# Closing the last attention run in two halves and feeding the residual into PSUM: two token-mixing layers on one Trainium2 core

## The chip, the cores and the metric

The kernel runs on one core of one Trainium2 chip. The core has five engines that work side by side and are held together by semaphores: PE (TensorE, the matrix unit, with its weight loads shown apart as PEld), DVE (VectorE), ACT (ScalarE), POOL (GpSimd) and SP (SyncE, which here only issues DMAs). The metric is the device time of one launch in microseconds, the median of several runs.

## The reference, cut to what matters

```python
S, D, H, F = 2048, 640, 32, 1536          # one sequence, heads of 20 columns

def A(x):                                  # attention on a layer-normed input
    q, k, v = heads(x @ wqkv)
    p = softmax(q @ k.T / sqrt(20))
    return heads_back(p @ v) @ wo

def B(x):                                  # a token-mixing MLP, along the sequence
    h = layernorm(x)
    u = gelu(einsum("sd,sf->df", h, w1) + b1)
    return (einsum("df,fs->ds", u, w2) + b2).T

x = A_x
x = x + A(layernorm(x));  x = x + B(layernorm(x))
x = x + A(layernorm(x));  x = x + B(layernorm(x))      # the same weights again
```

B mixes along the sequence: no row of its output is known before the last row of its input is. So each attention stage must be finished to the last token before the mixer's nonlinearity can start, and this happens twice, once per layer. The two layernorms in front of B are folded into one normalization with a slightly different epsilon (`twice=True`).

## The kernel before

**Attention.** The function `attention` runs once per layer. The 2048 queries are cut into blocks of 512, the 32 heads into 8 groups of 4 heads (one per 32 rows of PE). A *run* is one query block with one group; it consists of 16 *units*, each a stretch of 128 keys. For every unit PE makes the scores (tile `S`, line 643), ACT takes the exponential (tile `P`, line 705), and PE multiplies by V into the PSUM tile `acc` (line 1177), whose extra column holds the denominator. A part of the exponentials is computed on DVE instead of ACT, by integer tricks, in pairs of 512-column chunks (`ve_admit`, lines 542 to 602). Whether a pair is given to DVE is decided while the program is written out, by a planner that keeps estimated clocks of the engines and a DVE backlog; the result is a fixed order of instructions.

**The last query block** is worked in two halves of 256 queries. In its runs the 16 units are two times 8: units 0 to 7 belong to group 2g and write columns 0 to 255 of `acc`, units 8 to 15 belong to group 2g+1 and write columns 256 to 511 (function `spans`).

**Closing a run** (`finish_run`): DVE transposes `acc` (line 733), takes the reciprocal of the denominators (746), scales (749) and transposes back into `attnT` (755). There is a single `acc` bank, so the next run's products wait for the first of these four steps. After the last closing, `enqueue_outproj_last` multiplies `attnT` by `wo` (line 1006) and adds the residual on DVE into the SBUF tile `x1last` (line 1014). For the last half block the first three of its four pairs of groups are projected while attention still runs; only the last pair is left for after the end.

**Between attention and mixer.** `emit_ln2_staged` then normalizes the last two tiles of 128 tokens on DVE: two `bn_stats` each (lines 195, 196), `bn_aggr` (198), the variance plus epsilon (201), the power on POOL (206), and the application (882) into `h2_view`. Before that it makes ACT load the table for GELU (879). Meanwhile PE multiplies zeros (`zero_wave`, line 695), 18 waves of four matmuls, to stay busy.

**The mixer.** All but the last two token tiles have been multiplied by `w1` during attention, in groups of matmuls (line 921) whose results DVE copies out (930) and POOL adds up in DRAM by DMA (`uacc`, 938). `mixer_head` adds the rest: for each of 12 row tiles, PE multiplies the last two token tiles (line 1602, tile `um`), DVE adds the partial sum that SP loaded back from `uacc` (load 1587, addition 1605), ACT applies GELU (1608), and PE starts on the products with `w2` (1624, later 1615). In the first layer the loaded sums lie in `KT`, in the second in `ua`. SP's queue is served in order; in the second layer it holds, in this order, `w2s` for tiles 0 and 1, the loads of `ua` 0 to 7, `w2s` for tiles 2 and 3, the loads of `ua` 8 to 11, and then the residual `x1in`.

Of the kernel before, what the change touches and what calls it, by code (L numbers as in the profile page):

```python
# [12 lines left out]
BF16 = mybir.dt.bfloat16  # L13
F32 = mybir.dt.float32
# [9 lines left out]
D = 640  # L24
H = 32
DH = 20
# [39 lines left out]
HOLD = 3  # L66
WARM_WAVES = 18
LOG2E = 1.4426950408889634
# [9 lines left out]
def kernel(  # L78
# [108 lines left out]
    def setup_wo():  # L187
        for h in range(H):
            g, j = divmod(h, 4)
            nc.sync.dma_start(out=wo_pad[32 * j:32 * j + DH, g, :], in_=A_wo[h * DH:(h + 1) * DH, :])  # L190

    def ln_stats(src, twice=False):
        st = stat.tile([128, 2, nc.vector.BN_STATS_DIM], F32, name="bnst")
        half = D // 2
        nc.vector.bn_stats(out=st[:, 0, :], in_=src[:, 0:half])
        nc.vector.bn_stats(out=st[:, 1, :], in_=src[:, half:D])
        mv = stat.tile([128, nc.vector.BN_AGGR_DIM], F32, name="mv")
        nc.vector.bn_aggr(out=mv[:], in_=st[:])
        veps = stat.tile([128, 1], F32, name="veps")
        if twice:  # L200
            nc.vector.tensor_scalar(out=veps[:], in0=mv[:, 1:2], scalar1=1.0 + LN_EPS, scalar2=LN_EPS * LN_EPS,
                                    op0=ALU.mult, op1=ALU.add)
        else:
            nc.vector.tensor_scalar_add(out=veps[:], in0=mv[:, 1:2], scalar1=LN_EPS)
        rstd = stat.tile([128, 1], F32, name="rstd")
        nc.gpsimd.tensor_tensor(out=rstd[:], in0=veps[:], in1=mhalf[:], op=ALU.pow)
        return mv[:, 0:1], rstd[:, 0:1]

# [22 lines left out]
    def attention(st, x_in_ap, x_mid, uacc_l, feed, feed_stack):  # L231
# [165 lines left out]
        def new_run(qb, g, final, closed):  # L397
            run = dict(qb=qb, g=g, pending=[], done=0, closed=closed, final=final, acc=None)
            runs.append(run)
            return run  # L400
# [29 lines left out]
        def extend(now):  # L430
# [3 lines left out]
            if all(reach(qg, now) == NKT - ptr[qg] for qg in early_runs):  # L434
                early[0] = False
                for qg in sorted(early_runs, key=lambda qg: (cur is None or qg != (cur["qb"], cur["g"]), qg)):
# [11 lines left out]
                    run["final"] = run["closed"] = True  # L448
                for qg in order_left:
                    run = new_run(*qg, True, True)  # L450
                    for kt in range(NKT):
                        add_unit(run, kt)
                return True
            if cur is not None and reach((cur["qb"], cur["g"]), now) == 0:
# [262 lines left out]
        def finish_run(run):  # L717
# [3 lines left out]
            acc_free[0] = 1e9  # L721
            box = {}
            nth = part_no.get((qb, g), 0)
            whole = run["final"]
# [3 lines left out]
            def turn(end):  # L728
                if not whole and nth == 0:
                    box["T1"] = part_view((qb, g))  # L730
                else:
                    box["T1"] = ntmp.tile([128, 512], F32, name="T1")[:]
                nc.vector.transpose(out=box["T1"], in_=acc[:])  # L733
                acc_free[0] = end + DVE_TO_PE
# [8 lines left out]
            def recip(end):  # L743
                box["v"] = box["T1"].rearrange("p (c i) -> p c i", i=32)
                box["r"] = ntmp.tile([128, 16], F32, name="rden")
                nc.vector.reciprocal(out=box["r"][:], in_=box["v"][:, :, DH])

            def scaled(end):
                nc.vector.tensor_tensor(out=T2[:, :, 0:DH], in0=box["v"][:, :, 0:DH],
                                        in1=box["r"][:].unsqueeze(2).to_broadcast([128, 16, DH]), op=ALU.mult)  # L750

            def back(end):
                to = late["atp"].tile([128, 512], BF16, name="attnT")
                at_live[0] += 1
                nc.vector.transpose(out=to[:], in_=T2[:].rearrange("p c i -> p (c i)"))
                attnT_tiles.setdefault(qb, {})[g] = to

            def after(end):
                early_left.discard((qb, g))
                if qb >= LASTQB:  # L760
                    last = NG // 2 - 1
                    if qb == LASTQB and g == last:
                        enqueue_outproj_last(0, list(range(NG // 2)), end + DVE_TO_PE)
                    elif qb > LASTQB and g == last - 1:
                        enqueue_outproj_last(1, list(range(last)), end + DVE_TO_PE)
                    elif qb > LASTQB and g == last:
                        enqueue_outproj_last(1, [last], end + DVE_TO_PE)
                elif len(attnT_tiles[qb]) == NG:
                    enqueue_outproj(qb, end + DVE_TO_PE)
            rest = [(0.5, added, 0.0, True)] if nth else []  # L770
            if whole:
                rest += [(0.244, recip, 0.0), (0.49, scaled, 0.0, True), (0.71, back, 0.0)]
            ahead = [p for p in dvm["procs"] if p.rank in (0, 3) and getattr(p, "norm", False)]
            first = Proc(0, [(0.71, turn, 0.0)], at + PE_TO_DVE)

# [17 lines left out]
        hT_dead = [False]  # L793
        ln2_deferred = []
        N_KEYS = 2 * NQB * NG
# [60 lines left out]
        def do_ln2(tt, x1s, end):  # L856
            if tt >= NT - TAIL:
                ln2_deferred.append((tt, x1s))
                return

            def dst():
# [14 lines left out]

        def emit_ln2_staged(items):
            assert check_hT_dead()
            nc.scalar.activation(out=warm_act[:, 0:1], in_=mhalf[:, 0:1], func=ACT.Gelu_apprx_tanh, scale=1.0)
            stats = [ln_stats(x1s[:], twice=True) for (tt, x1s) in items]  # L880
            for (tt, x1s), (mean, rstd) in zip(items, stats):
                nc.vector.tensor_scalar(out=h2_view[:, tt, :], in0=x1s[:], scalar1=mean, scalar2=rstd,
                                        op0=ALU.subtract, op1=ALU.mult)

# [103 lines left out]
        def enqueue_outproj_last(half, pairs, ready):  # L988
            attnT = attnT_tiles[LASTQB + half]
            first, final = pairs[0] == 0, pairs[-1] == NG // 2 - 1  # L990
            tt0 = 4 * LASTQB + 2 * half
            if first:
                load_xin(tt0)
            if half == 0:
                mm1_prefetch(NQB - 2, 0)
            for ttl in range(2):
                tt = tt0 + ttl
                for ci, (c0, c1) in enumerate(((0, D // 2), (D // 2, D))):
# [3 lines left out]
                    for gi, (gp, odd) in enumerate(gs):  # L1002
                        def mm(t, gp=gp, odd=odd, gi=gi, ttl=ttl, c0=c0, c1=c1, w=w, ci=ci, tt=tt):
                            if first and gi == 0 and ci == 0 and ttl < 1:
                                load_xin(tt + 1)
# [6 lines left out]
                    def evac(t, end, eng, tt=tt, c0=c0, c1=c1, w=w, ci=ci):  # L1012
                        x1s = x1last[:, tt - 4 * LASTQB, :]
                        nc.vector.tensor_tensor(out=x1s[:, c0:c1], in0=t[:, 0:w],
                                                in1=tt_state[tt]["xin"][:, c0:c1] if first else x1s[:, c0:c1], op=ALU.add)
                        if first and ci == 1:
                            del tt_state[tt]
                        if final and ci == 1:
                            do_ln2(tt, x1s, end)
                    add_fill("O", 500.0, mms, evac, w, ready=ready)  # L1020
# [292 lines left out]
        assert not dvm["procs"] and not acm["procs"]  # L1313
        emit_ln2_staged(ln2_deferred)
        idle = pp["acc"].tile([128, 512], F32, name="acc")
# [422 lines left out]
```

## Time and profile before

| | |
|---|---|
| median of 3 runs | 1787.47 us (1786.66 to 1788.98) |
| the profiled execution | 1791.82 us, of which the span from first to last instruction is 1789.6 us |
| mean granted TensorE clock | 0.993 |
| PE busy | 1702.3 us, 95% of the span |
| ACT busy | 1680.8 us, 94%; of it 1640.2 us are exponentials (line 705) |
| DVE busy | 1542.4 us, 86% |
| POOL busy | 360.1 us, 20% |
| last exponential ends, first layer and second | 830.2 and 1716.8 us |
| first addition in the mixer's head (line 1605), first layer and second | 840.64 and 1727.37 us |

Times in the profile are counted from the first instruction of the profiled execution. A line of a timeline gives the start in us, the duration in us, the engine, the source line, the operation, what it writes and reads, and how often; in brackets stands the idle time of the engine before it and what ended that. A line of the windows view gives, for each stretch, its length, the busy time and the number of instructions of each engine, and then the granted clock of PE, the mean busy share of the 16 DMA engines, and GB/s. The DMA share counts packets in flight, so it can stand a little over 1.

### The profile page before, as it was taken

What the parts mean: (1) busy time and instruction counts of PE and PEld (TensorE: products, weight loads), DVE (VectorE), ACT (ScalarE), POOL (GpSimd) and SP (SyncE); (2) the same over time, 40 slices, a digit from 0 to 9 for tenths busy, and PEclk for the clock granted to TensorE, in tenths of its full rate; (3) what the DMA queues carried; (4) which work ended last, traced back from release to release, by engine and by line L of the source; (5) the groups of instructions that cost most, each with busy time, mean ns of one, the idle gap of its engine ahead of it and who ended that gap; (6) DMA issues with size and microseconds to landing.
All of it is one profiled execution on the core that took longest, in us unless ns stands there. A gap on an engine that the chain in (4) does not pass through costs nothing.

```text
span 1789.6 us, 42888 instructions
## 1 busy us (share of the span) xinstructions
PE 1702.3 (95%) x17880; PEld 669.4 (37%) x17880; DVE 1542.4 (86%) x2433; ACT 1680.8 (94%) x1508; POOL 360.1 (20%) x539
## 2 busy tenths in 40 slices
PE   8999999999999999999999998999999999999999
PEld 3333333333333344444533432333333333444445
DVE  7479999999999999998543478999999999899972
ACT  8999999999999999997789998999999999899960
POOL 3011111122233121231000011112223331212310
PEclk9999999999999999999999998999999999899999
DMA  4200000011225110057412100001212440101665
GB/s 121 27 1 1 1 2 2 23 51 55 70 53 93 21 46 2 10 88 202 140 50 73 61 1 1 1 2 38 65 49 82 85 73 2 61 2 36 100 212 180
DMA packets 110306, 97.56 MB, mean 55 GB/s; under 512 B 52128, under 2 KB 88608, under 8 KB 110112
## 3 DMA queue, kind: packets, MB, share of 16 engines
q1 hardware_dynamic: 97664, 71.22, 13.2%
q0 software_dynamic: 12448, 23.61, 7.9%
q8 instruction: 139, 2.28, 0.5%
q14 instruction: 55, 0.45, 0.1%
HBM read 55.48 MB, written 39.32 MB: 53 GB/s over the span
## 4 chain that ended last, share of the span: by engine, by line
ACT 48%; PE 24%; issue 21%; DVE 6%; DMA 1%; SPq 0%; POOL 0%; DVEq 0%; ACTq 0%; POOLq 0%
ACT P L705 48%; PE S L643 7%; PE acc L1177 3%; PE misc L921 2%; PE acc L695 2%; PE ya L1615 2%; PE misc L1028 1%; DVE ew L542 1%; DVE et L576 1%; DVE Pd L585 1%; PE um L1602 1%; PE ya L1624 1%; PE yb L1615 1%; DVE ey L572 1%; PE misc L968 0%
## 5 line engine op out<-in xcount | busy, mean ns | idle before, releaser
L705 ACT ACTIVATE P<-S 128x1024 bf16<-128x1024 f32 (+1 forms) x1450 | 1640.2, 1371 | 22.8 <-PE S L643 17.2
L643 PE MATMUL S<-QTq,KT 32*128 32x512 bf16 (+1 forms) x4528 | 589.0, 338 | 67.8 <-ACT P L705 51.2
L602 POOL TENSOR_SCALAR ey<-ew 128x512 f16<-128x512 uint16 x388 | 240.0, 618 | 1012.9 <-DVE et L576 417.7
L643 PEld LDWEIGHTS <-KT 32*128 32x128 bf16 x5144 | 234.4, 91 | 538.7 <-issue 514.2
L1177 PE MATMUL acc<-P,Vaug 128*32 128x512 bf16 (+1 forms) x4504 | 368.4, 346 | 2.5 <-DVE T L733 2.4
L542 DVE TENSOR_SCALAR ew<-Dt 128x512 int32<-128x512 f32 x474 | 323.5, 682 | 21.1 <-PE Dt L643 14.0
L695 PE MATMUL acc<-zr,zw 128*32 128x512 bf16 x4300 | 338.1, 385 | 1.2 <-POOL zr L151 1.2
L585 DVE SCALAR_TENSOR_TENSOR Pd<-ew,et 128x1024 int16<-128x1024 int16 x237 | 297.8, 1256 | 1.0
L576 DVE SCALAR_TENSOR_TENSOR et<-ey,ew 128x1024 f32<-128x1024 f16 x237 | 290.5, 1226 | 2.1
L643 PE MATMUL Dt<-QTq,KT 32*128 32x512 bf16 (+1 forms) x616 | 182.8, 333 | 0.0
L1177 PEld LDWEIGHTS <-Vaug 128*32 128x32 bf16 x5120 | 103.6, 94 | 179.8 <-issue 170.8
L572 DVE TENSOR_TENSOR ey<-ey 128x1024 f16<-128x1024 f16 x237 | 161.3, 681 | 6.1 <-POOL ey L602 1.5
L695 PEld LDWEIGHTS <-zw 128*32 128x32 bf16 x4448 | 112.0, 97 | 103.3 <-issue 59.9
L829 POOL TENSOR_TENSOR rstd<-veps,mhalf 128x1 f32<-128x1 f32 x60 | 51.4, 857 | 262.1 <-DVE veps L827 204.2
L1177 PE MATMUL acc<-Pd,Vaug 128*32 128x512 bf16 (+1 forms) x616 | 94.1, 338 | 0.0
L1028 PE MATMUL misc<-hh,wq_pad 128*128 128x512 bf16 x305 | 88.4, 383 | 0.1
L930 DVE COPY ustg<-misc 128x320 f32<-128x320 f32 x143 | 68.7, 481 | 10.1 <-PE misc L921 7.3
L968 PE MATMUL misc<-wo_pad,attnT 128*128 128x320 bf16 x384 | 73.6, 306 | 2.2 <-DVE xin L980 1.8
L921 PE MATMUL misc<-h2st,w1st 128*128 128x320 bf16 x384 | 74.6, 302 | 0.0
L921 PEld LDWEIGHTS <-w1st 128*128 128x128 bf16 x672 | 52.2, 97 | 58.6 <-issue 45.7
L733 DVE STREAM_TRANSPOSE T<-acc 128x512 f32<-128x512 f32 x79 | 55.9, 708 | 19.1 <-PE acc L1177 18.9
L1028 PE MATMUL misc<-hh,wk_pad 128*128 128x512 bf16 x240 | 70.7, 386 | 0.0
(135 smaller groups left out, 1141.3 us busy)
## 6 DMA issues: line engine op xcount, KB each, us to landing
uacc<-ustg POOLq DMA_DIRECT2D x72, 320.0 KB, 4.4
w2s<-in_B_w_dram SPq DMA_DIRECT2D x16, 768.0 KB
x1in<-xd SPq DMA_DIRECT2D x24, 320.0 KB
w1st<-in_B_w_dram SPq DMA_DIRECT2D x48, 128.0 KB
xd<-x2s SPq DMA_DIRECT2D x16, 320.0 KB
xin<-xd SPq DMA_DIRECT2D x16, 320.0 KB
w1st<-in_B_w_dram SPq DMA_DIRECT2D x24, 192.0 KB
xd<-x1s SPq DMA_DIRECT2D x12, 320.0 KB
```

The source lines that it names most:

```text
L542: nc.vector.tensor_scalar(out=w[:, slot, :], in0=Dt[:, :], scalar1=127.0 * FIX, scalar2=0.0, op0=ALU.add, op1=ALU.max)
L572: nc.vector.tensor_tensor(out=y, in0=y, in1=y, op=ALU.mult)
L576: nc.vector.scalar_tensor_tensor(out=box["t"][:, 0:512 * k], in0=ve_y.pop(p)[:, 0:512 * k], scalar=MANT_C * MANT_K ** 2, in1=frac, op0=ALU ...
L585: nc.vector.scalar_tensor_tensor(out=bits, in0=whole, scalar=128.0, in1=box["t"][:, 0:512 * k], op0=ALU.mult, op1=ALU.add)
L602: return engine.tensor_scalar(out=out_ap, in0=in_ap, scalar1=MANT_K / FIX, scalar2=-MANT_K * MANT_S, op0=ALU.mult, op1=ALU.add)
L643: pe(nc.tensor.matmul(out_ap[:, c0:c0 + w], lhsT=KT[32 * j:32 * j + 32, g, kt * 128:(kt + 1) * 128], rhs=get_QT(st, qb)[32 * j:32 * j + 32 ...
L695: pe(nc.tensor.matmul(bank[32 * j:32 * j + 32, :], lhsT=zw[:], rhs=zr[:].to_broadcast([128, 4, 128]), start=start, stop=stop, skip_group_c ...
L705: nc.scalar.activation(out=P[:, 0:ncs, :].rearrange("p a b -> p (a b)"), in_=St[:, 0:ncs, :].rearrange("p a b -> p (a b)"), func=ACT.Exp, ...
L921: pe(nc.tensor.matmul(t[:, 0:w], lhsT=w1_of[(p, ft)][:, sti, :], rhs=rows_in[sti][:, c0:c1], start=(sti == 0), stop=(sti == n_in - 1)))
L968: pe(nc.tensor.matmul(t[:, 0:w], lhsT=attnT[g][:, ttl * 128:(ttl + 1) * 128], rhs=wo_pad[:, g, c0:c1], start=(g == 0), stop=(g == NG - 1)))
L1028: pe(nc.tensor.matmul(t[:, :], lhsT=wpad[:, dt_, g, :], rhs=hT[:, dt_, tb * 512:(tb + 1) * 512], start=(dt_ == 0), stop=(dt_ == NDT - 1)))
L1177: pe(nc.tensor.matmul(acc[32 * j:32 * j + 32, a0:a0 + w], lhsT=Vaug[:, (kt * H + hh_) * VW:(kt * H + hh_) * VW + 32], rhs=P[:, slot, c0:c0 ...
```

## The change

Four edits, all at the end of each of the two attention stages.

- The last run is planned as two runs of 8 units. Each closes for itself, on its 256 columns of `acc`, `T1` and `attnT`; the first of them closes while the units of the second are still computed.
- The function `end_tiles` takes the place of the last projection's evacuation and of `emit_ln2_staged`. PE writes zeros into two tiles of PSUM (four waves), ACT copies the residual of the last two token tiles into them, and PE adds the eight matmuls of the last projection on top, in the order: even group, both token tiles; odd group, both token tiles.
- DVE's `bn_stats` read these sums in PSUM. ACT copies both sums back to SBUF, each behind the statistics of its tile, and applies the norm to the first of the two token tiles; DVE applies it to the second.
- The waves of zeros behind this go from 18 to 14.

```diff
-WARM_WAVES = 18
+WARM_WAVES = 14
...
-                for qg in order_left:
+                for qg in order_left[:-1]:
                     run = new_run(*qg, True, True)
                     for kt in range(NKT):
                         add_unit(run, kt)
+                for odd in range(2):
+                    run = new_run(*order_left[-1], True, True)
+                    run.update(c0=256 * odd, c1=256 * odd + 256)
+                    for kt in range(NKT // 2):
+                        add_unit(run, kt + odd * (NKT // 2))
...
-                nc.vector.transpose(out=box["T1"], in_=acc[:])
+                    box["T1"] = ntmp.tile([128, 512], F32, name="T1")[:, c0:c1]
+                nc.vector.transpose(out=box["T1"], in_=acc[:, c0:c1])
                 acc_free[0] = end + DVE_TO_PE
...
-                    elif qb > LASTQB and g == last:
-                        enqueue_outproj_last(1, [last], end + DVE_TO_PE)
...
-        def emit_ln2_staged(items):
-            assert check_hT_dead()
+        def end_tiles():
+            assert check_hT_dead() and TAIL == 2
             nc.scalar.activation(out=warm_act[:, 0:1], in_=mhalf[:, 0:1], func=ACT.Gelu_apprx_tanh, scale=1.0)
-            stats = [ln_stats(x1s[:], twice=True) for (tt, x1s) in items]
-            for (tt, x1s), (mean, rstd) in zip(items, stats):
-                nc.vector.tensor_scalar(out=h2_view[:, tt, :], in0=x1s[:], scalar1=mean, scalar2=rstd,
-                                        op0=ALU.subtract, op1=ALU.mult)
+            gp = NG // 2 - 1
+            attnT = attnT_tiles[LASTQB + 1][gp]
+            sums = [s_tile(w)[:].rearrange("p a b -> p (a b)") for w in (3, 2)]
+            for t in sums:
+                for c in (0, 512):
+                    zero_wave(t[:, c:c + 512], True, True)
+            for t, x1 in zip(sums, x1_end):
+                nc.scalar.copy(out=t[:, 0:D], in_=x1)
+            for odd in range(2):
+                for ttl, t in enumerate(sums):
+                    for c0, c1 in Y_CUTS:
+                        pe(nc.tensor.matmul(t[:, c0:c1], lhsT=attnT[:, 256 * odd + ttl * 128:256 * odd + (ttl + 1) * 128],
+                                            rhs=wo_pad[:, 2 * gp + odd, c0:c1], start=False, stop=(odd == 1),
+                                            skip_group_check=True))
...
+            def gather(i):
+                for k in range(2):
+                    nc.vector.bn_stats(out=st[i][:, k, :], in_=halves[i][k])
+                after_vector(nc.scalar.copy(out=x1_end[i], in_=sums[i][:, 0:D]))
+
+            def spread(i):
+                nc.vector.bn_aggr(out=mv[i][:], in_=st[i][:])
...
+                nc.gpsimd.tensor_tensor(out=rs[i][:], in0=v[:], in1=mhalf[:], op=ALU.pow)
+            gather(0)
+            spread(0)
+            gather(1)
+            shift = stat.tile([128, 1], F32, name="nmr")
+            nc.vector.tensor_scalar(out=shift[:], in0=mv[0][:, 0:1], scalar1=rs[0][:, 0:1], scalar2=-1.0,
+                                    op0=ALU.mult, op1=ALU.mult)
+            nc.scalar.activation(out=h2_view[:, NT - 2, :], in_=x1_end[0], func=ACT.Identity, bias=shift[:, 0:1],
+                                 scale=rs[0][:, 0:1])
+            spread(1)
+            nc.vector.tensor_scalar(out=h2_view[:, NT - 1, :], in0=x1_end[1], scalar1=mv[1][:, 0:1], scalar2=rs[1][:, 0:1],
+                                    op0=ALU.subtract, op1=ALU.mult)
...
-        emit_ln2_staged(ln2_deferred)
+        end_tiles()
```

## The prediction

> **What bounds the kernel now.** I read the page first: PE 95%, ACT 94%, DVE 86% busy, and of ACT's time 1640.2 us is exponentials. Such shares say little of an edit that touches two short stretches, so next came the timeline from the last exponential of each layer to the mixer's first additions. The second layer:
>
> ```profile
> 1717.40 0.72 DVE L733 STREAM_TRANSPOSE T<-acc 128x512 f32<-128x512 f32 x1 [0.53 <-PE acc L1177]
> ...
> 1719.73 0.45 PE L1006 MATMUL Dt<-wo_pad,attnT 128*128 128x320 bf16 x2 [2.40 <-DVE attnT L755]
> ...
> 1720.92 5.76 PE L695 MATMUL acc<-zr,zw 128*32 128x512 bf16 x72
> ...
> 1725.32 0.61 DVE L882 TENSOR_SCALAR hh<-x1last,mv,rstd 128x640 bf16<-128x640 f32 x1 [0.44 <-POOL rstd L206]
> 1726.61 1.26 PE L1602 MATMUL um<-hh 128*128 128x512 bf16 x8
> 1727.37 9.77 DVE L1605 TENSOR_TENSOR ua<-um,ua 128x640 f32<-128x640 f32 x12 [1.44 <-PE um L1602]
> ```
>
> From 1717.40 to 1725.93 it is one chain on DVE. Then PE, still at its zeros, starts `um` 0.7 us late. The first layer has the same chain, with `um` waiting for the norm itself:
>
> ```profile
> 830.99 0.99 PE L921 MATMUL Dt<-hh,w1st 128*128 128x320 bf16 x6
> ...
> 831.61 0.70 DVE L733 STREAM_TRANSPOSE T<-acc 128x512 f32<-128x512 f32 x1
> ...
> 839.51 0.61 DVE L882 TENSOR_SCALAR hh<-x1last,mv,rstd 128x640 bf16<-128x640 f32 x1 [0.44 <-POOL rstd L206]
> 840.17 0.97 PE L1602 MATMUL um<-hh 128*128 128x512 bf16 x6 [0.61 <-DVE hh L882]
> ...
> 840.64 9.77 DVE L1605 TENSOR_TENSOR KT<-um,KT 128x640 f32<-128x640 f32 x12 [0.52 <-PE um L1602]
> ```
>
> Then the windows view, for clock and DMA in these stretches:
>
> ```profile
> 830.21:833.62 3.41, 1.77 (x25) 0.85 (x22) 2.32 (x5) 1.49 (x3) 0.00 (x0) 1.00 1.08 290
> 1717.67:1721.09 3.42, 1.35 (x12) 0.82 (x16) 2.78 (x7) 0.64 (x2) 0.36 (x1) 1.00 1.08 343
> 1721.09:1724.50 3.41, 3.41 (x36) 1.33 (x32) 3.27 (x12) 0.00 (x0) 0.63 (x2) 0.50 1.05 294
> 1730.00:1734.00 4.00, 4.00 (x31) 2.27 (x30) 3.94 (x6) 3.94 (x6) 0.00 (x0) 1.00 1.07 377
> ```
>
> The zeros of the second layer ran at clock 0.50 for 3.41 us, right behind a stretch in which PE was busy 1.35 of 3.42 us (39%). In the first layer the thinnest such stretch had 1.77 us (52%) and no drop. And the DMA share is over 1 through all of the second layer's tail. What those DMAs are, SP's queue tells:
>
> ```profile
> 1715.88 5.21 SPq L1587 DMA_DIRECT2D ua<-uacc  x8
> 1721.54 0.63 SPq L1637 DMA_DIRECT2D w2s<-in_B_w_dram  x1
> 1723.80 5.94 SPq L1587 DMA_DIRECT2D ua<-uacc  x4
> ```
>
> SP is held back here: each issue waits for the landing eight issues earlier. By the completion marks of the loads' semaphores in the trace, `ua` 0 lands at 1721.52, `ua` 7 at 1729.98, and the four behind `w2s` at 1733.48, 1734.31, 1735.14 and 1735.96. Their additions (12 back to back in 9.77 us) start at 1733.87, 1734.68, 1735.49 and 1736.31. So the last four loads land 0.35 to 0.39 us before they are needed. In the first layer the last load lands at 846.29 for an addition at 849.58: 3.3 us ahead.
>
> **The change, part by part.**
>
> *Half closing.* The four steps took 0.72, 0.25, 0.49 and 0.71 us, 2.17 in all. A one-column row of DVE (`veps`) takes 0.15, so I call 0.15 the fixed part: 0.43 + 0.24 + 0.32 + 0.43 = 1.42 us. `attnT` comes 0.75 us earlier, at 1719.0 instead of 1719.73.
>
> *The residual by ACT.* The second layer's last exponential ends at 1716.80; the GELU table load (1.28) and its dummy (0.20) end at 1718.32. PE's four waves of zeros (18 took 4.07 us at full clock: 0.23 each) run from 1717.3 to 1718.2, in time. A copy of 640 f32 columns from SBUF to PSUM has no row. Above lies ACT's Identity of 640 columns (0.92), below the slope of the exponentials (0.43 per 512 columns, with 0.06 fixed: 0.60); the nearest in kind is ACT's copy of 640 bf16 columns out of PSUM, 0.69, which I take. Two copies end at 1719.7 (1719.5 to 1720.2). PE's order holds the odd group's matmuls behind the even group's on both tiles, so they start at 1720.05, a microsecond after `attnT` is there: behind the shortened closing it is ACT that is late.
>
> *No evacuation on DVE.* Four additions (0.48 each, 1.7 us overlapped) go. The first tile's sums stand at about 1720.5 instead of 1721.1, the second's 0.3 behind instead of at 1721.9. `bn_stats` from PSUM has no row. From SBUF it takes 0.48; a DVE addition of 320 columns with one operand in PSUM (L1014) takes 0.48, and one of 336 from SBUF alone (L741) 0.51, so I see no price for PSUM and take 0.48. [...]
>
> *The norm.* From 1720.5: two statistics to 1721.4, aggregate and epsilon (0.21, 0.15) to 1721.85, POOL's power (0.56) to 1722.5. The second tile's statistics run beside that to 1722.65, `shift` (0.21) follows, then aggregate and epsilon to 1723.25, power to 1723.9, application (0.61) to 1724.6. ACT: copy back to 1722.2, second copy back (behind the second statistics) to 1723.4, Identity (0.92) to 1724.3. What is queued behind ACT's waiting copies is only this Identity, and it ends ahead of DVE's. So both tiles stand at 1724.6 instead of 1725.93: 1.3 us earlier. Fourteen waves from 1720.6 at full clock end at 1723.8, ahead of that, so PE's 0.7 us go too: `um` starts at 1724.65 instead of 1726.61, 2.0 us earlier.
>
> *First layer.* A leftover group of `L921` holds PE to 831.98, and the zeros come behind it, to 832.9. The copies end at 834.0, the odd matmuls' first tile at 834.8; with the same 4.1 us behind it the norm stands at 838.9 instead of 840.12. **Gain 1.2 us**; its loads have 3.3 us to give, so it reaches the products with `w2` whole, and everything after moves with it.
>
> *Second layer, what of the 2.0 arrives.* Its DMAs start when the last scores are done (SP waits for `S`), which the change does not move. Addition 8 can start at 1733.5 and the last at 1736.0 instead of 1736.31: **0.3 us**. The rest becomes a new wait of DVE for `ua` 8.
>
> *The closing put into the stream.* The first half now closes while exponentials run: about 1.4 us of DVE near 1703, where DVE is fully busy (no idle of over 0.06 us from 1686 to 1709). PE's wait for `acc` costs ACT nothing that I see: none of the eight run changes I looked at left ACT idle. But a fuller backlog can keep one pair of chunks from DVE; ACT then takes two chunks more, 0.43 us each. The second layer's last pair is admitted at 1704.8, just behind the new closing; the first layer's stands earlier relative to its end. Between 0 and 0.85 us per layer; I take **0.4 in all**.
>
> Sum: -1.2 - 0.3 + 0.4 = **-1.1 us**. The profiled execution took 1791.82 us (2.2 outside its span of 1789.6), 4.35 above the median of 1787.47; there it gives 1790.7 and a span of 1788.5, and on the median **1786.4**.
>
> **The rivals.**
>
> *Both heads arrive whole.* If the loads are faster where nothing is recorded (the profiled run is 0.24% slow), the second layer gives 2.0: -1.2 - 2.0 + 0.4 = -2.8, 1784.7. If the leftover `L921` group also moves into the new pause of the stream, the first layer's zeros start at 831.1, its copies end 0.9 earlier: -3.7, and without a lost pair -4.1, 1783.4. For it speaks a margin as thin as 0.35 us; against it, 7.1 MB in 21.5 us with all 16 engines filled.
>
> *No gain arrives.* Both layers lose a pair (+1.7): 0.2 over, 1787.7.
>
> *The new wait lets the clock fall (slower).* While DVE waits 1.8 us for `ua` 8, PE has nothing but zero to two `um` tiles, so it is idle some 1.8 us of a 3.41 us stretch, 47% busy: between the 39% that was followed by half a clock and the 52% that was not. It decides when the busy share falls under a value between these and the stretch lies badly. At half clock PE, which from there on is the chain to the end, loses 1.7 us: +0.6, 1788.1; with two lost pairs +1.9, 1789.4. The record shows also a drop of 10.2 us at 1540, which would cost 5. [...]
>
> **How the numbers follow.** Forecast 0.50, both heads whole 0.26, no gain 0.12, clock falls 0.12. A difference of 0.2% is 3.6 us, about what a measurement of this kernel can tell from no change (its three runs lie 2.3 us apart). Over that on the fast side: most of the second case's better half and a little of the first, 0.20. On the slow side: the long drop, or drops with other work displaced, 0.11. Within: 0.69. The range takes the second case nearly to its end and the slow one to its middle: 1783.6 to 1789.0; the forecast's own, by the copies' bounds and 0 to 1.7 for the pairs, is 1785.6 to 1788.0.
>
> **What would show it.** Right: DVE's addition in the second layer waits for a DMA of `ua`, about 1.8 us before the ninth; the first addition stands 8.4 us behind the last exponential instead of 10.6 there, 9.2 instead of 10.4 in the first layer; PE's odd matmuls wait for ACT's copies, not for `attnT`; the clock is 1.00 behind the closing. Wrong: no DMA wait and a head of 9.8 us moved whole (the second case); an exponential stretch that ends over 1 us later, more ACT exponentials than 1450 by columns (the third); a stretch at 0.50 behind 1731 (the fourth).

## The result, and the profile after

The changed kernel took **1792.18 us** (median of 20 executions, 1789.17 to 1794.24), the kernel before on the same chip 1788.13: a ratio of **1.0021, 95% interval 1.0014 to 1.0027**. It is slower by some 3.7 us, where I had forecast 1.1 us less, and the median lies 3.2 us above the end of my range.

The profiled execution of the changed kernel took 1789.54 us, the third shortest of the 20; a second one, profiled later, took 1793.47. The one of before was long for its kernel (1791.82), partly by a stretch of 10.2 us at half clock at 1540, in the middle of the second layer, which the change does not touch. Every profiled execution here, of whatever kernel, also has 3.4 to 13.7 us at half clock between 1081 and 1105 (that of before 10.2, that of the changed kernel 13.7). So the spans are not compared here, only the stretches behind each layer's last exponential. That exponential ends at 830.25 and 1712.34 in the changed kernel.

The first layer in the timeline of the changed kernel:

```profile
826.58 0.89 POOL L961 DMA_DIRECT2D uacc<-ustg  x1 [8.91 <-DVE ustg L953]
...
830.63 0.99 PE L944 MATMUL Dt<-hh,w1st 128*128 128x320 bf16 x6
...
831.46 0.98 PE L944 MATMUL S<-hh,w1st 128*128 128x320 bf16 x6
...
832.37 0.62 PE L683 MATMUL S<-zr,zw 128*32 128x512 bf16 x8
...
833.84 0.49 DVE L953 COPY ustg<-Dt 128x320 f32<-128x320 f32 x1 [1.56 <-DMA uacc<-ustg]
834.24 0.48 DVE L953 COPY ustg<-S 128x320 f32<-128x320 f32 x1
834.78 0.62 PE L683 MATMUL S<-zr,zw 128*32 128x512 bf16 x8 [1.79 <-DVE ustg L953]
...
835.44 0.70 ACT L873 COPY S<-x1last 128x640 f32<-128x640 f32 x1 [1.66 <-PE S L683]
836.19 0.98 PE L877 MATMUL S<-wo_pad,attnT 128*128 128x512 bf16 x6 [0.42 <-ACT S L873]
837.00 0.90 DVE L887 BATCH_NORM_STATS2 bnst<-S 128x6 f32<-128x320 f32 x2 [2.27 <-PE S L877]
...
841.56 0.82 DVE L1626 TENSOR_TENSOR KT<-um,KT 128x640 f32<-128x640 f32 x1 [0.71 <-PE um L1623]
```

There are now two leftover groups of products with `w1` (line 921 before, 944 now) instead of one, and the second of them sits in a tile of `S`. Its tile is wanted again at once: the zeros under the second token tile's sum are written into it. The groups are the two halves of the last row of partial sums, and DVE copies such a row into one of the two buffers `ustg`, from which POOL's DMA adds it to `uacc`. The buffer's previous DMA, issued at 826.58, has not landed. So DVE's copy waits 1.56 us for it (833.84), the zeros wait for the copies, ACT's second residual for the zeros, the odd matmuls for that residual, and the statistics for the odd matmuls (2.27 us idle on DVE). The first addition is 11.3 us behind the last exponential; it was 10.4 and I had it at 9.2. What is lost here arrives whole: from the end of the first layer's last addition to the second layer's last exponential it takes 859.8 to 862.3 us in all seventeen profiles other than that of before (866.4, with its 10.2 us at half clock), though that addition ends anywhere from 18.5 to 27.0 us behind the layer's last exponential.

The second layer, same view:

```profile
1712.72 0.99 PE L944 MATMUL Dt<-hh,w1st 128*128 128x320 bf16 x6
1712.84 0.45 DVE L724 STREAM_TRANSPOSE T<-acc 128x256 f32<-128x256 f32 x1 [0.71 <-PE acc L1198]
...
1715.72 0.97 PE L877 MATMUL S<-wo_pad,attnT 128*128 128x512 bf16 x6 [0.19 <-ACT S L873]
1716.53 0.90 DVE L887 BATCH_NORM_STATS2 bnst<-S 128x6 f32<-128x320 f32 x2 [1.79 <-PE S L877]
...
1720.36 1.25 PE L1623 MATMUL um<-hh 128*128 128x512 bf16 x8 [0.52 <-ACT hh L902]
1721.10 6.51 DVE L1626 TENSOR_TENSOR ua<-um,ua 128x640 f32<-128x640 f32 x8 [0.71 <-PE um L1623]
...
1729.47 0.82 DVE L1626 TENSOR_TENSOR ua<-um,ua 128x640 f32<-128x640 f32 x1 [1.87 <-DMA ua<-uacc]
1730.35 0.70 PE L1623 MATMUL um<-hh 128*128 128x512 bf16 x4 [1.70 <-DVE ua L1626]
```

Here the new end does what it should, and the first addition is 8.8 us behind the last exponential instead of 10.6. Then the ninth addition waits 1.87 us for `ua` 8, and PE waits 1.70 us with it. The windows view (columns as before) shows what follows:

```profile
1728.08:1731.50 3.42, 1.54 (x11) 0.75 (x9) 1.46 (x2) 1.22 (x2) 0.00 (x0) 1.00 1.03 392
1731.50:1734.91 3.41, 3.17 (x13) 1.50 (x13) 1.83 (x3) 2.48 (x3) 0.00 (x0) 0.50 1.09 344
```

PE was busy 1.54 of 3.42 us (45%), and the next 3.41 us ran at clock 0.50. From the last exponential to the end of the span it is 75.0 us instead of 72.8. SP's queue, in its own timeline:

```profile
1711.40 6.75 SPq L1608 DMA_DIRECT2D ua<-uacc  x8
1718.62 0.38 SPq L1658 DMA_DIRECT2D w2s<-in_B_w_dram  x1
1719.49 6.25 SPq L1608 DMA_DIRECT2D ua<-uacc  x4
```

The four last loads of `ua` stand behind a load of `w2s` whose product comes later. In the kernel before this order cost little, with the last loads 0.35 us ahead of need; now it decides.

### The profile page after: what moved, and what is told of

Read it like the earlier page. It is cut to its first block, busy times and chain, and to the rows that moved or that the text cites. A ratio compares the mean times of both kernels' runs of the same rounds, so it can differ in the third digit from the quotient of the medians.

```text
span 1787.3 us, 42954 instructions
## 1 busy us (share of the span) xinstructions
PE 1702.0 (95%) x17900; PEld 669.8 (37%) x17900; DVE 1538.1 (86%) x2433; ACT 1687.5 (94%) x1518; POOL 358.4 (20%) x539
## 3 DMA queue, kind: packets, MB, share of 16 engines
q1 hardware_dynamic: 97664, 71.22, 13.2%
## 4 chain that ended last, share of the span: by engine, by line
ACT 51%; issue 22%; PE 21%; DVE 3%; DMA 2%; SPq 1%; POOL 0%; DVEq 0%; ACTq 0%; POOLq 0%
ACT P L693 51%; PE S L631 6%; PE acc L1198 3%; PE ya L1636 2%; PE misc L944 2%; PE acc L683 2%; PE misc L1049 1%; DMA ua<-uacc 1%; PE yb L1636 1%; PE ya L1645 1%; PE misc L1552 0%; PE Dt L1552 0%; PE um L1623 0%; DVE et L564 0%; DMA uacc<-ustg 0%
## 5 line engine op out<-in xcount | busy, mean ns | idle before, releaser
L693 ACT ACTIVATE P<-S 128x1024 bf16<-128x1024 f32 (+1 forms) x1450 | 1639.8, 1376 | 17.9 <-PE S L631 13.9
L724 DVE STREAM_TRANSPOSE T<-acc 128x512 f32<-128x512 f32 (+1 forms) x81 | 56.3, 695 | 19.4 <-PE acc L1198 19.2
L1049 PE MATMUL misc<-hh,wk_pad 128*128 128x512 bf16 x240 | 71.2, 388 | 0.0
```

What stands on the lines that cost most here:

```text
L693: nc.scalar.activation(out=P[:, 0:ncs, :].rearrange("p a b -> p (a b)"), in_=St[:, 0:ncs, :].rearrange("p a b -> p (a b)"), func=ACT.Exp, ...
L1049: pe(nc.tensor.matmul(t[:, :], lhsT=wpad[:, dt_, g, :], rhs=hT[:, dt_, tb * 512:(tb + 1) * 512], start=(dt_ == 0), stop=(dt_ == NDT - 1)))
```

## The experiments

Ratios are against the kernel before on the same chip, with 95% intervals. "First addition" is its start behind the layer's last exponential, "end" the time from the second layer's last exponential to the end of the span, both from the profiled execution. Before: 10.4, 10.6 and 72.8 us.

**Which part costs.** One kernel has the half closing alone (old projection, evacuation, norm and 18 waves), the other the new end alone:

```diff
-        end_tiles()
+        emit_ln2_staged(ln2_deferred)
```

> The kernel before with the last run split in two and nothing else: the old evacuation, the old norms, 18 waves. Theory A (the split pushes one group of matmuls with w1 per layer behind the end, and in the first layer its copy to ustg waits for a DMA): the first layer has two such groups behind its last product, as after has, and its first addition of the head stands about 10.8 us behind the last exponential (before 10.4, after 11.3); in the second layer one group behind the end, and from the last exponential to the end of the span 72.5 to 72.8 us (before 72.8, after 75.0), for the head is hardly earlier than before and DVE waits little for ua. Sum 0 to +0.4 us. Theory B (it is the new end with its two passes over ACT that is slow): both stretches 0.5 us shorter than before or better, sum -1 us.

```diff
-                for qg in order_left[:-1]:
+                for qg in order_left:
                     run = new_run(*qg, True, True)
...
-                for odd in range(2):
-                    run = new_run(*order_left[-1], True, True)
...
```

> After without the split: one run of 512 columns, closed in four steps of 2.2 us, then the new end. Theory A: one group left behind the first layer's last product, as before, none in the second; the first addition of the first layer's head 9.2 to 9.4 us behind the last exponential, -1.1 us; the second layer's head is early and waits for ua 8, 72.5 us to the end if the clock holds, 74.2 or more with a stretch at 0.50 behind the wait. Sum -1.4, or +0.5 with the clock's drop. Theory B (the new end itself is slow): the first layer's stretch is 11 us or more, as in after; sum +3.

Half closing alone: 1790.83 us, **1.0013 (1.0004 to 1.0022)**, end 73.4 us, ninth addition 2.08 us late. Its profile has the two leftover groups in the first layer, a wait of 1.24 us for the landing, and the first addition at +10.3, where I expected 10.8. But that execution, 1786.74 us, was the shortest of eleven by over 2 us, so its stretches do not show where the median's 2 to 3 us go, and the sum of 0 to +0.4 that I expected was too small.

New end alone: 1785.57, **0.9986 (0.9977 to 0.9995)**; first additions +8.8 in the first layer and +8.9 in the second, end 72.1. The loss comes with the half closing, and the new end by itself is a gain. The two do not add up: +0.13% and -0.14% alone, +0.21% together, so most of the loss needs both. The timeline of the new end alone, first layer:

```profile
830.73 0.49 DVE L948 COPY ustg<-misc 128x320 f32<-128x320 f32 x1 [2.00 <-DMA uacc<-ustg]
830.82 0.99 PE L939 MATMUL Dt<-hh,w1st 128*128 128x320 bf16 x6
831.74 1.05 PE L678 MATMUL S<-zr,zw 128*32 128x512 bf16 x16
```

There is one leftover group. The wait for the landing is there too (2.00 us), but at the first half of the last row, ahead of the closing, and the zeros follow the leftover group in one go.

**Where the second leftover group lies.** With the tail's groups in `misc` and `Dt` alone, the zeros find both `S` tiles free:

```diff
-            if tail_no[0] % 4 == 0:
...
-            return s_tile(w)[:, 0, :]
+            return (Dbank if tail_no[0] % 2 == 1 else misc).alloc()
```

> After, with the leftover groups of matmuls put into the two small PSUM tiles alone (misc and Dt), so that the tiles for the sums are free when the zeros come. Theory A: the second pair of zero waves waits no longer for DVE's copy of the leftover group; only DVE's two copies (until 834.7) stand ahead of the statistics; the first layer's first addition 9.3 to 9.6 us behind the last exponential instead of 11.3; the second layer as in after, 75.0 with the drop of the clock. Sum against after -1.8 us, against before +1.2. If it is the new end by itself (B), the first layer stays at 11 us.

1788.99 us, 1.0002 (0.9993 to 1.0011). The copy waited 3.04 us here, and still the first addition stood at +10.4 (I expected 9.3 to 9.6): PE no longer waits, and only the statistics behind the copies in DVE's queue do. End 73.7, with the ninth addition 2.69 us late.

**The order in SP's queue.** All twelve loads of `ua` ahead of the second load of `w2s`:

```diff
-        for ft in range(8):
+        for ft in range(NF):
             load_ua(ua[ft], uacc_l, ft)
...
-        for ft in range(8, NF):
-            load_ua(ua[ft], uacc_l, ft)
```

> After, with SP's queue in the second mixer changed in one place: the second block of w2s is loaded behind all twelve ua instead of behind eight. Theory A (DVE waits 1.9 us for ua 8 to 11, PE runs dry, and the clock falls to half for 3.4 us): ua 8 to 11 land some 2.3 us earlier, no DMA wait of line 1605's additions, no stretch at 0.50 behind them; from the last exponential to the end of the span 70.8 to 71.5 us instead of 75.0; the first layer stays at 11.3. Sum against after -3.7 us, against before -1. Rival (the second w2s is needed as early as it came, or the DMA engines' bytes set the end whatever their order): the products of tile 2 wait for w2s, and the stretch stays at 73 us or more.

1788.17 us, 0.9998 (0.9989 to 1.0007): about 4 us under the changed kernel. The end is 71.1 us, without a wait for `ua` and without a stretch at half clock. The first layer is as it was (+11.3). Its executions fall into two groups, five at 1785.5 to 1786.7 and six at 1788.2 to 1789.9.

The same edit on the kernel before, as a control:

> The kernel before with that order of the loads alone. Its additions start 0.35 to 0.39 us behind the landing of ua 8 to 11, so with the old end there is next to nothing to win: 72.1 to 72.8 us from the last exponential to the end (before 72.8), depending on whether the zeros run at half clock; the first layer unchanged at 10.4. Sum 0 to -0.5 us. If it gains over 1 us, then the loads held the kernel before as well, and e4's gain was not one over the change's own wait.

1787.69 us, 0.9999 (0.9990 to 1.0008), end 71.9. The 0.9 us under the 72.8 are not the order's: that profile has no stretch at half clock in the second layer's zeros, and the kernel before with another edit, in the last experiment below, ends at 72.0 without one. Its first layer did not stay at +10.4 but stood at +11.0, with half clock at 834.69. So the order is worth some 4 us to the changed kernel and nothing that can be told to the one before. With the order and the leftover groups in `misc` and `Dt`, on the changed kernel, and with the order on the new end alone:

> e3 and e4 together: the sums' tiles kept free of leftover groups, and the second w2s behind all ua. The split is still in. First layer 10.4 us from the last exponential to the first addition, as in e3 (before 10.4); second layer 71.1 us to the end, as in e4 (before 72.8). Against before -1.7 us, one cluster of runs, since PE is idle less in both places. If the two parts depend on each other (the groups left over need the order of the loads), less than that.

> e2 and the order of e4: no split, the new end, the second w2s behind all ua. First layer 8.8 us to the first addition as in e2 (before 10.4); second layer no wait for ua 8 (0.9 us in e2) and 71.1 to 71.4 us to the end (e2 72.1, before 72.8). Against before -3.2 us, against e2 -0.8. If the wait for ua cost nothing in e2 (theory: the PE-bound products with w2 behind it take it up), the same as e2.

1785.51 us, 0.9989 (0.9980 to 0.9997), and 1785.20, 0.9988 (0.9979 to 0.9998).

**Filling PE's wait in the first layer** with eight waves of zeros into an unused bank, on top of the order:

```diff
             for t in sums:
+                if layer == 0 and t is sums[1]:
+                    keep = pp["acc"].tile([128, 512], F32, name="acc")
+                    for _ in range(8):
+                        zero_wave(keep, True, True)
```

> e4 (after with the second w2s behind all ua) with one addition in the first layer's end: PE multiplies 8 more waves of zeros into acc between the zeros for the first sum and those for the second, where it now stands idle 1.8 us. Nothing else moves: the second pair of zeros still waits for DVE's copy. Theory C (the timed runs of e4 fall in two clusters, 1785.5 to 1786.7 and 1788.2 to 1789.9, because that idle time of PE at times falls into one stretch of 3.41 us and the clock is halved in the first layer's head): profile as e4's (first addition 11.3 us behind the last exponential, 71.1 us from the last exponential to the end), but the timed runs lose the upper cluster, median 1785.5 to 1786.5. If the clusters come from elsewhere, both stay and the median is 1788 again.

1786.57 us, 0.9997 (0.9989 to 1.0006). PE ran the zeros until 835.24, paused 1.90 us behind them, and its clock stayed at 1.00 (the odd matmuls took 0.98 us), but the copy happened to wait 3.39 us in the profiled execution and the first addition stood at +13.2: against the changed kernel's first profile, 1.83 us more of wait and 1.84 us more to the first addition. So no half clock followed here, and the landing was as late as without the zeros. Nine of the eleven executions lie at 1785.6 to 1787.5, two at 1788.5 and 1791.3, so this does not settle what makes the upper group. The changed kernel itself, profiled once more, shows a late landing too:

> After once more, for a second profile of the same program. Theory D: the wait of DVE's copy for the landing (1.56 us in the first profile) differs by a microsecond or more, and the first layer's first addition (11.3 us behind the last exponential) moves by as much; the second layer waits 1.9 to 2.1 us for ua 8 again, and its stretch is 75.0 us with a halved clock behind the wait or 73.0 to 73.7 without, as in e1 and e3.

```profile
835.56 0.49 DVE L953 COPY ustg<-Dt 128x320 f32<-128x320 f32 x1 [3.10 <-DMA uacc<-ustg]
...
836.50 0.62 PE L683 MATMUL S<-zr,zw 128*32 128x512 bf16 x8 [3.33 <-DVE ustg L953]
...
837.91 1.48 PE L877 MATMUL S<-wo_pad,attnT 128*128 128x512 bf16 x6 [0.42 <-ACT S L873]
```

1793.47 us; first addition +13.9 instead of +11.3, with a stretch at half clock at 838.2. The same program, the same order, and the first addition 2.6 us later: the wait for the landing is 1.5 us longer, and the rest is the half clock that follows PE's pause (the odd matmuls took 1.48 us instead of 0.98).

**Taking the landing away, into memory that another load waits for.** The last row is staged in a tile of the residual's pool instead of `ustg`: on the changed kernel, on the one with the new order, and on the new end alone with the new order.

```diff
-                            rows[ft] = late["ustg"].tile([128, D], F32, name="ustg")
+                            last_row = p == len(M_GROUPS) - 1 and ft == NF - 1
+                            rows[ft] = (late["xsp"].tile([128, D], F32, name="xin" if x_in_ap.dtype == F32 else "x1s")
+                                        if last_row else late["ustg"].tile([128, D], F32, name="ustg"))
```

> After with one edit: the last row of the partial sums (the one whose matmuls the split pushes behind the end) is staged in an idle residual tile instead of in one of the two ustg buffers, so that DVE's copy of the leftover group has no DMA to wait for. The order of all instructions is the same. Theory D (the first layer lost its gain, and the timed runs a varying 2 to 3 us, to DVE's wait for that DMA's landing, 1.56 us in after's profile and 3.39 in e10's, with the zeros, the second sum and the statistics behind it): no DMA wait of the copy to the last row, first addition of the first layer 9.5 to 9.9 us behind the last exponential instead of 11.3, and in the timed runs 2 to 4 us less than after, median 1788 to 1790. Rival (the leftover matmuls themselves, or PE's and ACT's order in the new end, hold the first layer): 11 us or more remain.

> e4 (after, second w2s behind all ua) with the spare row. Theory D: first layer 9.5 to 9.9 us, second layer 71.1 us to the end; the timed runs in one cluster, none of e4's upper one (1788.2 to 1789.9): median 1784.5 to 1785.5. If e4's clusters are made by PE's clock in the first layer, as supposed for e10, and not by the DMA: PE's idle time there also shrinks with the wait, so this run alone does not part the two; the clock's records of its profile and of the others have to.

> The best version so far (e8: new end without the split, second w2s behind all ua) with the spare row. In e8's profile DVE's copy of the last row stood 1.86 us for a DMA, just ahead of the closing. Theory D: the closing starts up to 0.3 us earlier, behind the copy; first layer 8.3 to 8.8 us (e8 8.8), second 71.1 us; against before -3.3 us. If that copy was hidden by the last products, the same as e8.

All three were slower, against my expectation: 1795.67 (1.0043, 1.0029 to 1.0056), 1792.38 (1.0025, 1.0017 to 1.0034) and 1793.41 (1.0033, 1.0023 to 1.0043). In the first, DVE's copy waits for nothing and the first addition stands at +9.6; but the last of the twelve ends at +27.0 instead of +21.1. SP's queue says why:

```profile
829.30 5.67 SPq L1610 DMA_DIRECT2D KT<-uacc  x8
843.37 0.38 SPq L1660 DMA_DIRECT2D w2s<-in_B_w_dram  x1
843.85 2.24 SPq L1610 DMA_DIRECT2D KT<-uacc  x4
```

The first layer's load of `w2s` is issued at 843.37; in the changed kernel, at 824.11. It goes into memory that the residual's pool gives up, so it now waits for the row's DMA (8.4 us), and the last four loads of `KT` wait behind it. The runs tell nothing of the landing's price.

**Taking it away with a place nobody waits for**: the row goes into a part of `hh` that is unused at that time.

```diff
-                            rows[ft] = late["ustg"].tile([128, D], F32, name="ustg")
+                            last_row = p == len(M_GROUPS) - 1 and ft == NF - 1
+                            rows[ft] = (hh[:, NL_ * F:NL_ * F + 2 * D].bitcast(F32) if last_row
+                                        else late["ustg"].tile([128, D], F32, name="ustg"))
```

> The changed kernel, but the very last row of w1's partial sums is staged in an unused part of hh instead of in one of ustg's two buffers, so that its copy waits for no landing, and (unlike the spare tile before) no load of w2 waits on that memory. Landing theory: DVE's copy of the first leftover row has no DMA wait (1.6 to 3.1 us in the changed kernel), the first addition of the first layer stands 9.5 to 9.9 us behind its last exponential instead of 11.3 to 13.9, the last one at +19.4, SP's loads of w2 stay at 824 to 826; the second layer's end as in the changed kernel (73 to 75 us); median 2 to 3 us under the changed kernel's, some 1789 to 1790. Rival (the zeros and copies are late for a reason of their own, the landing only fills time that would be lost anyway): the first addition stays behind +10.8, median within 1 us of the changed kernel's 1792.

1788.50 us, 0.9995 (0.9985 to 1.0005), 3.7 us under the changed kernel's median; first addition +9.6, the end of the last at +19.4 instead of +21.1. The timeline:

```profile
834.40 0.45 DVE L955 COPY hh<-Dt 128x320 f32<-128x320 f32 x1
...
834.56 1.35 PE L683 MATMUL S<-zr,zw 128*32 128x512 bf16 x16
834.77 0.47 DVE L955 COPY hh<-S 128x320 f32<-128x320 f32 x1
```

The copies follow the closing's last transpose without a wait, and the zeros stand in one row with hardly a pause. The end is as bad as before (75.3, `ua` 8 late by 2.64 us, half clock at 1731.6): the two losses are separate. Both removed, on the changed kernel and on the new end alone, and the row alone on the kernel before:

> As the run before, and in the mixer w2's second load is issued behind all loads of ua. Both theories of the loss together: first addition +9.6 in the first layer, no wait for ua and no half clock at the second layer's end (71.1 us), and a single cluster of times at 1784.5 to 1785.5, against two clusters (1785.5 to 1786.7, 1788.2 to 1789.9) with the second load's place alone. Rival: the two clusters stay, since they come from elsewhere; median 1788.

> The new end without the half closing, w2's second load behind all of ua, and the row in hh. There is one leftover group and it is released early anyway (first addition +8.8): 8.3 to 8.8, second end 71.2 us; median 1784.5 to 1785.5, no more than the same kernel without the row in hh (1785.2), and none of its executions at 1788. Rival: the same times as without the row, with one in ten at 1788 or more.

> The kernel before with only that row in hh. Landing theory: its one leftover copy was released by a landing that came about 0.5 us late, and the closing's chain on DVE stands behind it for little: first addition +10.0 to +10.4 (was +10.4), median 0 to 1 us under the kernel before. Rival (the landing costs the kernel before as much as the changed one): 2 us or more under it.

1784.75 us, **0.9976 (0.9967 to 0.9986)**; 1784.20, **0.9975 (0.9966 to 0.9984)**; 1786.65, 0.9988 (0.9978 to 0.9998). The first has one group of executions, 1783.3 to 1786.8: without the wait for the landing, the upper group is gone. The waits for the landing behind a half closing lie in two groups as well, 1.24 to 1.57 us in three profiles and 2.86 to 3.39 in four. That the slower executions are those with the longer wait is likely but not shown, since none of the upper group was profiled. The second layer of the first kernel:

```profile
1720.15 9.83 DVE L1628 TENSOR_TENSOR ua<-um,ua 128x640 f32<-128x640 f32 x12 [0.70 <-PE um L1625]
```

Twelve additions back to back, end 71.2 us. The kernel before paid the landing too, 1.3 us by the medians against the 0 to 1 that I expected: its copy at 831.20 held the closing's first step, and the first addition goes from +10.4 to +9.6 without it. The new end with both repairs has the lowest median measured here, and the half closing adds nothing to it that can be told.

## Why the prediction was wrong, point by point

**First layer, -1.2: the step that failed.** I wrote that a leftover group holds PE to 831.98 "and the zeros come behind it". That is the kernel before's one group, and I priced no wait behind it. The change alters the order of the stream, one group more is left, and it takes a tile that the new end needs. The profiled executions show +0.9 and +3.5 us, not -1.2. A hint of the copy's wait was in the trace of before:

```profile
831.20 0.49 DVE L930 COPY ustg<-misc 128x320 f32<-128x320 f32 x1 [2.69 <-PE acc L1177]
```

This copy of the same row came 0.1 us behind the landing of a `uacc` DMA at 831.08, though its row names PE; and my list of who waits for whom never got to the copies of the leftover groups. Without the landing the layer gives -0.8 (+9.6); without the half closing as well, -1.7 (+8.8). The kernel before without its own landing stands at +9.6 too, so measured against that the whole change gives this layer nothing, and the new end alone 0.8. So even without that wait, the half closing costs 0.9 us here instead of bringing its 0.75. The closing itself is as I had it (0.45, 0.20, 0.33 and 0.45 us, 1.43 against 1.42; the 0.24 for the reciprocal should have been 0.20 by my own rule), and `attnT` is there 0.74 us earlier. But with two leftover groups PE's zeros start 2.12 us behind the last exponential instead of 1.31 with one, and the sums wait for the copies behind the zeros.

**The closing put into the stream, +0.4.** The term counted pairs of exponentials lost by DVE. None was: 474 chunks on DVE and 1450 exponentials on ACT in both kernels. What the earlier closing displaced was a group of products with `w1` in each layer, which I had not priced. In the second layer the last accumulating DMA is issued 2.71 us behind the last exponential instead of 0.37.

**Second layer, -0.3: the rival was right.** The head itself came out nearly as worked out, 8.8 instead of 8.4: the sums waited for ACT's copies (0.70 and 0.69 against 0.69), two statistics took 0.90, the Identity 0.92. The copies came late, because here too a leftover group stood ahead of PE's zeros: these ended 2.4 us behind the last exponential (I had 1.4), and the copies at 3.3 instead of 2.9. The wait for `ua` 8 came too, 1.87 against 1.8. But I let the ninth addition start no later than `ua` landed before, and had the clock hold. In the six profiles with the half closing and the old order of loads, the ninth addition starts 17.1 to 18.1 us behind the last exponential; with the new end alone it is 16.3, and it was 17.1 before, when nothing waited. So nothing of the 0.3 arrives. That the later `uacc` DMA is what delays `ua` was only argued, not tried. Then the clock fell, the case to which I gave 0.12: in the three profiles with a drop behind the wait the end took 75.0 to 75.4 us, against 73.4 to 74.0 in the three with such a wait and no drop (half closing alone, free `S` tiles, and the spare residual tile). By these, the drop is some 1.5 us (I had 1.7) and the late loads the rest, 0.6 to 1.2 over before. My condition for the drop, a busy share under some value between 39% and 52%, is not borne out as it stands: 45% was followed by one, 42 to 44% in two other kernels was not.

**The sum.** Forecast -1.2, -0.3, +0.4; measured +0.9 to +3.5, +2.2 to +2.6 and 0. By the ratios, taking one loss away is worth 0.26% (row in `hh`) or 0.23% (order of loads), both 0.45%, and the change without both stands at -0.24%, just past the fast end of the case "both heads arrive whole" that I gave 0.26. The range failed because each rival broke one step, and here a step of each layer broke for a reason of its own; the first layer's, a displaced group that waits for a buffer, was in none of them.

**Statistics from PSUM, and the clock.** The statistics from PSUM took 0.90 us a pair, as I had it; before, from SBUF, the pair ran from 836.01 to 836.88, 0.87. So the four cost 0.06 us more than from SBUF, where I saw no price. As to the clock, a stretch of 3.42 us that was 45% busy was followed by 3.41 us at half clock; with the half closing alone, one of 3.40 us that was 44% busy (1.49 us) was followed by 3.60 us at 1.00.

## What to carry to other kernels

When an edit shortens a chain at the end of a stage, list what the program's own order will leave over behind that stage, and for each leftover the tile it sits in, the buffer its copy needs, and the DMA that must land first. If a head moves earlier by more than its loads' margin, move the loads first: the order of SP's queue was worth nothing to the kernel before and about 4 us to the changed one. When a buffer is borrowed to take a wait away, look at what is loaded into that memory next.

## What the runs showed of the hardware

- The accumulating DMA of one row (320 KB) lands a median of 4.4 us after its issue over the whole program, but at the end of the changed kernel's first layer, where SP's loads of `KT` run from 828.48 on, up to 7.3 us (issued at 826.58, and the copy that waits for it starts at 833.84) and in another execution of the same program up to 8.8 (826.76, and 835.56).
- Half clock does not follow from PE's pause alone. Waits of DVE for `ua` of 1.87, 2.64 and 2.70 us, with pauses of PE of 1.70, 2.48 and 2.53, were followed by 3.4 us at 0.50; waits of 2.08, 2.69 and 2.82 us in three other kernels, with pauses of 1.92, 2.53 and 2.65, were not. The clock's changes in a trace lie whole multiples of 3.41 us apart (before: 1, 1, 2, 130, 3, 50, 1 and 19 of them; the changed kernel: 4, 186, 1 and 15). In the stretch of 3.41 us, laid out from these changes, that holds the end of the pause, PE was busy 45%, 27% and 36% before a drop, and 44%, 42% and 48% where none came. So the busy share does not part them cleanly either; what does stays open.
- ACT copies 640 f32 columns from SBUF to PSUM in 0.70 us and back in 0.69: here the direction made no difference.
